# Attention and a two-layer product on one core: second exp sums moved ahead of the first-product tiles, and three smaller moves

## The chip, the cores and the metric

One core of a Trainium2 chip. The metric is device time in microseconds of one execution; before, three runs took 422.45, 422.8 and 423.35 us, a median of 422.8. The core's engines are TensorE (PE in the profile; its weight loads are PEld), VectorE (DVE), ScalarE (ACT), GpSimd (POOL) and SyncE (SP), which here only issues transfers. Each runs its own instructions in order, and they wait for each other by semaphores.

## What is computed

```python
# q, k, v: (8 batches, 12 heads, 448 tokens, 64)
scores = (1 / sqrt(64)) * q @ k.T
m = max(scores); e = exp(scores - m)
attn = e / (sum(e) + exp(-m) + 1e-9)
x = (attn @ v) laid out as (8 * 448 tokens, 768)
h = x @ w_in            # (3584, 2048), the "first product"
g = max(h, 0) ** 2
out = g @ w_out         # (3584, 768), the "second product"
```

The kernel leaves the maximum out of both halves of the fraction, so that it is exp(scores) / (1 + sum(exp(scores))); the 1e-9 is left out too. The sums over the keys are matmuls with a column of ones ("row sums"), after VectorE has added the four chunks of keys together.

## The kernel before

Heads go in pairs, six to a batch. Batches 0 and 1 are worked pair by pair; from batch 2 on two pairs make a cycle, three cycles a batch. In a cycle TensorE does the scores of two pairs (`ua`, `ub`), between them pieces of the second product of an earlier batch (`rows`), then the values of the cycle before, then tiles of the first product of the batch before (`run(ins, ...)`), and among them the row sums of its own two pairs. ScalarE takes the exps and the reciprocals (as exp(-ln)). VectorE adds the exp chunks, normalises the values into `xt`, and takes each first-product tile out of PSUM (maximum with 0 into `rt`, L296; square into `gs`, L298).

```python
def cast(b, pr):
    for name in "qk":
        f = flat.tile([P, 2, RUN, D], FP16, name=f"flat{name}")
        nc.vector.tensor_copy(f, naturals[name, b, pr])                     # L145
        naturals[name, b, pr] = f

def transposes(b, pr):
    tp = mp_tile(FP16)
    for i, name in enumerate("qk"):
        ...  # eight TensorE transposes each                                # L153
    nc.vector.tensor_copy(qks[b][:, 0:2, pr * S:(pr + 1) * S], tp[:, :, 0:S])   # L157

def add_chunks(u, et, es, half, step):       # for n == S
    e = et.rearrange("p (k x) -> p k x", k=RUN)
    if step < 2:
        nc.vector.tensor_add((es, half[:, 0:2 * S])[step], e[:, 2 * step], e[:, 2 * step + 1])  # L207
    else:
        nc.vector.tensor_add(es, es, half[:, 0:2 * S])                      # L209

def mp_tile(dtype=FP32):     # three buffers of m_psum and one of x_psum, in turn
    if joined[0] >= 0:
        joined[0] += 1
    pool, name = (x_psum, "xp") if joined[0] > 0 and joined[0] % 4 == 0 else (m_psum, "mp")
    return pool.tile([128, 512] if dtype == FP32 else [128, 2, 512], dtype, name=name)
```

`row_sums` takes such a tile, does two matmuls per unit into it (L243), and ScalarE's Ln (L246) and Exp (L247) make the reciprocals. `values` (L229) and `tile_in` (L279, 12 half-array matmuls per 128 columns of `w_in`) take such tiles too. `tile_out` does 384 output columns of 128 tokens in 16 matmuls (L326 split by rows, L281 on the whole array); ScalarE or VectorE takes them out, and SyncE stores them.

The start, where three and four warming matmuls (`keep_warm`, L420) stand around the first scores:

```python
keep_warm(9)
cast(0, 0)
transposes(0, 0)
keep_warm(3)
cast(0, 1)
for i in range(2 * NPAIR):
    ...
    scores(u, et, 0)
    if i == 0:
        keep_warm(4)
```

Batch 1's last part sets how much first product each of its pairs drains; `left()` is what is still queued:

```python
        if first:
            queue(FIRST, S - FIRST)
            share[0] = left() / (NPAIR + 0.9)
```

A cycle from batch 2 on:

```python
        scores(ua, ea, 0); rows(11)
        scores(ua, ea, 1)
        add_chunks(ua, ea, sa, ha, 0)
        rows(11)
        scores(ub, eb, 0)
        add_chunks(ua, ea, sa, ha, 1); add_chunks(ua, ea, sa, ha, 2)
        rows(10)
        scores(ub, eb, 1)
        add_chunks(ub, eb, sb, hb, 0)
        for at in pending:                 # the two pairs of the cycle before
            ...
            xp = mp_tile()
            values(units[at], ets.pop(at), xp)
            normalise([units[at]], xp, rcps.pop(at))
        if b in ON_PE and pr + 2 < NPAIR:  # batch 2 alone, here
            transposes(b, pr + 2)
            transposes(b, pr + 3)
        if pr == 0:
            run(ins, len(ins))
            queue((b - 1) * S, S)
            if b > 2:
                run(outs)
            ...  # transfers for the next batches
        n = (3, 7, 6)[pr // 2]
        early = (0 if b > 2 else 2) if pr == 0 else 3
        if pr:
            run(ins)                       # one tile
        add_chunks(ub, eb, sb, hb, 1)
        add_chunks(ub, eb, sb, hb, 2)
        run(ins, early - (pr > 0))
        for at in (i, i + 1):
            rcps[at] = row_sums([units[at]], (ess.pop(at)[0:1],))
        run(ins, n - early)
```

Of the kernel before, what the change touches and what calls it, by code (L numbers as in the profile page):

```python
# [10 lines left out]
AF = mybir.ActivationFunctionType  # L11
# [4 lines left out]
def kernel(  # L16
# [9 lines left out]
    nc = tc.nc  # L26

    B, H, S, D = q.shape
    NT, DM = out.shape
    DF = moe_w_in.shape[1]  # L30
    NPAIR = H // 2
    DCH = DM // 128
    NFFB = DF // 128
# [4 lines left out]
    HALF = DM // 2  # L38
# [36 lines left out]
    whole, vns, qks, xts, naturals, stages = {}, {}, {}, {}, {}, {}  # L75
# [66 lines left out]
    def cast(b, pr):  # L142
        for name in "qk":
            f = flat.tile([P, 2, RUN, D], FP16, name=f"flat{name}")
            nc.vector.tensor_copy(f, naturals[name, b, pr])  # L145
            naturals[name, b, pr] = f

    def transposes(b, pr):
        tp = mp_tile(FP16)
        for i, name in enumerate("qk"):  # L150
            for s in range(RUN):
                for h in range(2):
                    nc.tensor.transpose(tp[64 * h:64 * h + 64, i, P * s:P * s + P],  # L153
                                        naturals[name, b, pr][:, h, s, :], ident[0:P, 0:P])
        if b not in qks:
            qks[b] = qk_pool.tile([128, 3, COLS], FP16, name="qk")
        nc.vector.tensor_copy(qks[b][:, 0:2, pr * S:(pr + 1) * S], tp[:, :, 0:S])  # L157

# [41 lines left out]
    def add_chunks(u, et, es, half, step):  # L202
        n = u[3]
        if n == S:
# [5 lines that stand above are left out]
        elif step == 1:  # L210
            nc.vector.tensor_add(half[:, 0:4 * n], et[:, 0:4 * n], et[:, 4 * n:8 * n])
        elif step == 2:
            f = half[:, 0:4 * n].rearrange("p (h j n) -> p h j n", h=2, j=2)
            nc.vector.tensor_add(es[:, 0:2 * n].rearrange("p (h n) -> p h n", h=2), f[:, :, 0, :], f[:, :, 1, :])
# [35 lines left out]
    def normalise(us, xp, rcp):  # L250
        b, pr, q0, n = us[0]
        if b not in xts:
            xts[b] = xt_pool.tile([128, DCH, S], FP16, name="xt")
        if len(us) == 1:
            nc.vector.tensor_mul(xts[b][:, pr, q0:q0 + n], xp[:, 0:n], rcp[:, 0:n])
        else:
            two = [t[:, 0:2 * n].rearrange("p (j n) -> p j n", j=2) for t in (xp, rcp)]
            nc.vector.tensor_mul(xts[b][:, pr:pr + 2, q0:q0 + n], *two)
# [51 lines left out]
            nc.sync.dma_start(out=rows[t, p:p + m, :], in_=ot[o:o + m, n0:n1])  # L310
            c += m

    def tile_out(tok, n0):

        w = HALF
        if n0 == 0:
            ots[tok] = osb_pool.tile([128, DM], FP32, name="ot")
        ot = ots[tok]
        rows = mode[0] == ROWS2
        op = mp_tile()  # L320
        lo = mp_tile() if rows else None
        for fb in range(NFFB):
            g = gs[:, fb, tok % RING:tok % RING + 128]
            if rows:
                for x, o in ((0, op), (64, lo)):
                    nc.tensor.matmul(o[:, 0:w], g[x:x + 64], wout[x:x + 64, fb, n0:n0 + w],  # L326
                                     start=(fb == 0), stop=(fb == NFFB - 1))
            else:
                product(op[:, 0:w], g, wout[:, fb, n0:n0 + w], start=(fb == 0), stop=(fb == NFFB - 1))
            if fb < NFFB - 1:  # L330
                yield w / 2.4
        if rows and n0 == 0:
            nc.vector.tensor_scalar(out=ot[:, n0:n0 + w], in0=op[:, 0:w], scalar1=OUT_SCALE, scalar2=None, op0=ALU.mult)
        else:
            nc.scalar.activation(out=ot[:, n0:n0 + w], in_=op[:, 0:w], func=AF.Copy, scale=OUT_SCALE)  # L335
        if rows:
            nc.vector.scalar_tensor_tensor(out=ot[:, n0:n0 + w], in0=lo[:, 0:w], scalar=OUT_SCALE,  # L337
                                           in1=ot[:, n0:n0 + w], op0=ALU.mult, op1=ALU.add)
        last = tok + 128 == NT
        if n0 or last:  # L340
            store(tok, ot, n0 if last else 0, n0 + w)
        yield w / 2.4

# [25 lines left out]
    ins, outs = [], []  # L369
    groups = [0]  # L370
# [8 lines left out]
    def complete(upto):  # L379

        while groups[0] + 128 <= upto:
            for n0 in (0, HALF):
                ns = NFFB * HALF / 2.4
                outs.append([ns, ns, tile_out(groups[0], n0)])
            groups[0] += 128

    def left():
        return sum(t[0] for t in ins)
# [9 lines left out]
    def drain(ns):  # L398
        while ins and ns > 0:
            ns -= one(ins)  # L400

    def run(tiles, n=1):
        for _ in range(min(n, len(tiles))):
            for _ in tiles.pop(0)[2]:
                pass
# [16 lines left out]
    share = [0.0]  # L422
# [67 lines left out]
    for i in range(2 * NPAIR, 3 * NPAIR):  # L490
        u, et, es, half = begin(i)
        prev = units[i - 1]
        first = i == 2 * NPAIR
        if not first:
            xp = x_psum.tile([128, 512], FP32, name="xp")
        mode[0] = COLS2
        scores(u, et, 0)
        if i in transpose_at:
            transposes(*transpose_at[i])
        if i == 2 * NPAIR + 2:  # L500
            load_natural(2, 3, 6)
            for j in range(2):
                load_wout(HALF, j, 2)
            load_v(2, 0, 6)
            stage(3)
        drain(left() * 0.5 if first else share[0] * 0.45)
        scores(u, et, 1)
        if first:
            done = units[i - 2:i]
            values(prev, ets.pop(i - 1), xp, prev[3])  # L510
            rcp = row_sums(done, (ess.pop(i - 2)[0:1], ess.pop(i - 1)[0:1]))
        else:
            done = [prev]
            rcp = row_sums(done, (ess.pop(i - 1)[0:1],))
            values(prev, ets.pop(i - 1), xp)
        drain(share[0] * 0.15)
        for step in range(3):
            add_chunks(u, et, es, half, step)
            drain(share[0] * (0.15, 0.1, 0.15)[step])
        if i == 3 * NPAIR - 1 and ins and ins[0][0] < ins[0][1]:  # L520
            run(ins)
        normalise(done, xp, rcp)
        if first:
            queue(FIRST, S - FIRST)
            share[0] = left() / (NPAIR + 0.9)

# [11 lines left out]
    for c in range((NU - 3 * NPAIR) // 2):  # L540
        i = 3 * NPAIR + 2 * c
        b, pr = units[i][0:2]
        new = []
        for j in range(2):
            new.append(begin(i + j))
        (ua, ea, sa, ha), (ub, eb, sb, hb) = new
        scores(ua, ea, 0)
# [5 lines that stand above are left out]
        add_chunks(ua, ea, sa, ha, 1)  # L553
        add_chunks(ua, ea, sa, ha, 2)
# [3 lines that stand above are left out]
        mode[0] = COLS2  # L558
        for at in pending:
            if at not in rcps:  # L560
                rcps[at] = row_sums([units[at]], (ess.pop(at)[0:1],))
            xp = mp_tile()
            values(units[at], ets.pop(at), xp)
            normalise([units[at]], xp, rcps.pop(at))
        if b in ON_PE and pr + 2 < NPAIR:
            transposes(b, pr + 2)
            transposes(b, pr + 3)
# [5 lines that stand above are left out]
            if b + 1 < B:  # L573
                transposed_loads(b + 1)
                hold(b + 1)
                load_v(b + 1, 0, NPAIR)
                if b + 2 < B:
                    stage(b + 2)
        n = (3, 7, 6)[pr // 2]
        early = (0 if b > 2 else 2) if pr == 0 else 3  # L580
        if pr:
            run(ins)
        add_chunks(ub, eb, sb, hb, 1)
        add_chunks(ub, eb, sb, hb, 2)
        run(ins, early - (pr > 0))
        for at in (i, i + 1):
            rcps[at] = row_sums([units[at]], (ess.pop(at)[0:1],))
        run(ins, n - early)
        if pr == NPAIR - 2:
            complete(b * S)  # L590
        pending = [i, i + 1]
# [38 lines left out]
```

The softmax here doesn't subtract the row's maximum and nothing guards it: scores larger than these inputs give would overflow.

## Time and profile before

| what | value |
|---|---|
| time, median of three | 422.8 us |
| span of the profiled execution | 420.5 us |
| attention cycles (batch 2 to 7) | about 68 to 358 us |
| last batch's products alone | about 358 to 417 us |
| TensorE's granted clock | 1.00 in every stretch |
| last store, issued and landed | 417.5, about 419 us |

The page gives busy time by engine, the chain of work that ended last, and groups of instructions by source line. The trace behind it gives single instructions with start and duration, and for each idle stretch of an engine the instruction that ended it. An arrow `<-` in a tile's name separates what is written from what is read. `64*112` ahead of a shape is the part of the 128 x 128 array that a matmul uses; two such matmuls on different halves run side by side. A matmul's drawn end lies past the next one's start, since matmuls are pipelined.

### The profile page before, as it was taken

The numbers are of one execution on the slowest core, as the hardware profiler recorded it, in microseconds if no ns is written. First come the engines' busy times: TensorE is split into PE (matmuls) and PEld (weight loads), VectorE is DVE, ScalarE is ACT, GpSimd is POOL, SyncE is SP. The second block draws the span as 40 slices with busy tenths as digits, with TensorE's granted clock in tenths as the row PEclk, the third lists the DMA queues.
The fourth block names the chain that finished last, engine by engine and source line by source line (L and its number), as shares of the span: only waits on it lengthen the run. The fifth ranks groups of instructions, "written<-read, shape, count | busy, mean of one in ns | idle before, by whom it ended". The sixth has DMA issues, their size and how long they took to land.

```text
span 420.5 us, 10659 instructions
## 1 busy us (share of the span) xinstructions
PE 408.4 (97%) x4705; PEld 259.9 (62%) x4705; DVE 280.2 (67%) x535; ACT 237.8 (57%) x327; POOL 36.2 (9%) x58
## 2 busy tenths in 40 slices
PE   8889999899999999999999999999999999999996
PEld 3567666566666666666666666666666666655663
DVE  4769888677864967668766768568676669287000
ACT  3998997755566464764675664673666665100111
POOL 7523310020000200002000300001000000000000
PEclk9999999999999999999999999999999999999999
DMA  9999999889109940299409960198101101010222
GB/s 205 197 197 198 200 202 199 156 142 175 38 19 207 179 107 2 75 204 169 104 2 181 175 136 19 39 203 138 40 2 39 39 2 39 38 39 0 76 75 76
DMA packets 75679, 45.58 MB, mean 108 GB/s; under 512 B 42544, under 2 KB 71856, under 8 KB 75312
## 3 DMA queue, kind: packets, MB, share of 16 engines
q0 software_dynamic: 28848, 22.16, 34.6%
q1 hardware_dynamic: 46064, 22.05, 23.1%
q10 hardware_dynamic: 720, 0.69, 0.6%
q8 instruction: 37, 0.61, 0.6%
q14 instruction: 10, 0.08, 0.1%
HBM read 45.69 MB, written 17.93 MB: 151 GB/s over the span
## 4 chain that ended last, share of the span: by engine, by line
PE 82%; DVE 11%; ACT 5%; issue 1%; ACTq 0%
PE mp L279 20%; PE mp L326 17%; PE mp L281 10%; PE sp L194 6%; PE mp L229 5%; PE xp L279 5%; PE xp L326 5%; DVE rt L296 4%; PE xp L281 4%; ACT et L162 3%; PE xp L229 3%; PE sp L182 3%; DVE es L209 2%; DVE half L207 2%; PE mp L420 1%; DVE gs L298 1%
## 5 line engine op out<-in xcount | busy, mean ns | idle before, releaser
L162 ACT ACTIVATE et<-sp 112x896 f16<-112x896 f32 (+2 forms) x192 | 166.0, 914 | 61.5 <-PE sp L194 44.2
L279 PEld LDWEIGHTS <-win 128*64 128x64 f16 x1536 | 90.6, 110 | 43.3 <-issue 7.4
L279 PE MATMUL mp<-xt,win 128*64 128x448 f16 (+2 forms) x1248 | 111.8, 324 | 2.8 <-DVE rt L296 1.2
L326 PE MATMUL mp<-wout,gs 64*128 64x384 f16 x864 | 102.3, 323 | 0.0
L296 DVE TENSOR_SCALAR rt<-mp 128x448 f16<-128x448 f32 (+2 forms) x100 | 62.2, 622 | 28.1 <-PE mp L279 16.0
L326 PEld LDWEIGHTS <-gs 64*128 64x128 f16 x1152 | 56.0, 94 | 31.9
L298 DVE TENSOR_TENSOR gs<-rt 128x448 f16<-128x448 f16 (+2 forms) x128 | 50.2, 392 | 4.4
L326 PE MATMUL xp<-wout,gs 64*128 64x384 f16 x288 | 52.6, 323 | 0.0
L246 ACT ACTIVATE rcp<-mp,one_b 128x448 f32<-128x448 f32 (+2 forms) x39 | 24.5, 629 | 36.1 <-PE mp L243 36.1
L335 ACT ACTIVATE ot<-mp 128x384 f32<-128x384 f32 x28 | 13.8, 492 | 52.5 <-PE mp L281 41.5
L207 DVE TENSOR_TENSOR es<-et 112x896 f16<-112x896 f16 x42 | 26.0, 620 | 17.7 <-ACT et L162 17.7
L194 PE MATMUL sp<-qk 64*112 64x224 f16 x480 | 33.8, 260 | 0.0
L281 PEld LDWEIGHTS <-gs 128*128 128x128 f16 x240 | 23.4, 98 | 15.8 <-issue 0.4
L194 PEld LDWEIGHTS <-qk 64*112 64x112 f16 x480 | 26.3, 128 | 9.7 <-issue 5.4
L279 PE MATMUL xp<-xt,win 128*64 128x448 f16 x288 | 31.5, 353 | 0.5 <-DVE rt L296 0.5
L229 PEld LDWEIGHTS <-vn 112*64 112x64 f16 x432 | 22.3, 109 | 15.0 <-issue 5.1
L281 PE MATMUL mp<-wout,gs 128*128 128x384 f16 x176 | 29.4, 326 | 0.0
L337 DVE SCALAR_TENSOR_TENSOR ot<-mp,ot 128x384 f32<-128x384 f32 x26 | 14.5, 558 | 21.8 <-PE sp L194 13.5
L247 ACT ACTIVATE rcp<-rcp 128x448 f32<-128x448 f32 (+2 forms) x48 | 27.7, 577 | 1.5
L209 DVE TENSOR_TENSOR es<-es,half 112x896 f16<-112x896 f16 x42 | 26.3, 625 | 1.4
L207 DVE TENSOR_TENSOR half<-et 112x896 f16<-112x896 f16 x42 | 25.9, 617 | 0.3 <-ACT et L162 0.3
L182 PE MATMUL sp<-qk 64*112 64x448 f16 (+2 forms) x192 | 24.0, 321 | 1.9 <-ACT et L162 1.4
(60 smaller groups left out, 310.9 us busy)
## 6 DMA issues: line engine op xcount, KB each, us to landing
vn<-in_v_dram POOLq DMA_DIRECT2D x7, 672.0 KB, 8.0
out_dram<-ot SPq DMA_DIRECT2D x9, 384.0 KB, 2.9
win<-in_moe_w_in_dram POOLq DMA_DIRECT2D x8, 384.0 KB, 13.8
wout<-in_moe_w_out_dram POOLq DMA_DIRECT2D x4, 768.0 KB, 12.9
stage_q<-in_q_dram POOLq DMA_DIRECT2D x4, 676.0 KB, 10.6
stage_k<-in_k_dram POOLq DMA_DIRECT2D x4, 676.0 KB, 13.6
out_dram<-ot SPq DMA_DIRECT2D x8, 288.0 KB, 2.6
out_dram<-ot SPq DMA_DIRECT2D x10, 192.0 KB, 2.7
```

What stands on the lines that cost most here:

```text
L162: nc.scalar.activation(out=out_, in_=in_, func=AF.Exp, scale=scale)
L182: nc.tensor.matmul(sp[:, h, o:o + n], qk[r, 1, x + P * kk:x + P * kk + P], qk[r, 0, x + q0:x + q0 + n], start=True, stop=True)
L194: nc.tensor.matmul(sp[:, odd, h * (S // 2):(h + 1) * (S // 2)], qk[r, which, kx:kx + 2 * P - 1:2], qk[r, 0, x:x + S // 2], start=True, sto ...
L207: nc.vector.tensor_add((es, half[:, 0:2 * S])[step], e[:, 2 * step], e[:, 2 * step + 1])
L209: nc.vector.tensor_add(es, es, half[:, 0:2 * S])
L229: nc.tensor.matmul(xp[64 * h:64 * h + 64, o:o + n], vns[b][:, 2 * pr + h, kk, :], of_head(chunk(et, u, kk // 2, kk), u, h), start=(kk == 0 ...
L247: nc.scalar.activation(out=rcp[:, 0:m], in_=rcp[:, 0:m], func=AF.Exp, scale=-1.0)
L279: nc.tensor.matmul(out_[x:x + 64], lhsT[:, x:x + 64], rhs, start=start, stop=stop)
L281: nc.tensor.matmul(out_, lhsT, rhs, start=start, stop=stop)
L296: nc.vector.tensor_scalar(out=rt[:, 0:m], in0=hp[:, 0:m], scalar1=0.0, scalar2=None, op0=ALU.max)
L298: nc.vector.tensor_mul(gs[:, f0:f0 + per, t0 % RING:t0 % RING + n], r, r)
L326: nc.tensor.matmul(o[:, 0:w], g[x:x + 64], wout[x:x + 64, fb, n0:n0 + w], start=(fb == 0), stop=(fb == NFFB - 1))
```

## The change

Four edits. In a cycle, the second pair's last two adds (`add_chunks(ub, ..., 1)` and `2`) move to right behind the normalises, ahead of the qk copies and of every product tile; where a tile stood ahead of them, it now goes with the others, so that three tiles come before the row sums as before. At the seam from batch 1 to batch 2, batch 1's pairs drain a smaller share of the first product, so that a tile is left for the first cycle of batch 2, and that cycle does one new tile instead of two ahead of its row sums. At the start, ScalarE casts the first k while VectorE casts the first q, and the first copy of transposed q and k is made in two halves. At the end, the last 384 output columns are made as 256 and 128, each with its own copy and store.

```diff
@@ cast
-            nc.vector.tensor_copy(f, naturals[name, b, pr])
+            if b == 0 and pr == 0 and name == "k":
+                nc.scalar.activation(out=f, in_=naturals[name, b, pr], func=AF.Copy)
+            else:
+                nc.vector.tensor_copy(f, naturals[name, b, pr])
@@ transposes
-        nc.vector.tensor_copy(qks[b][:, 0:2, pr * S:(pr + 1) * S], tp[:, :, 0:S])
+        parts = (0, S // 2, S) if b == 0 and pr == 0 else (0, S)
+        for x, y in zip(parts, parts[1:]):
+            nc.vector.tensor_copy(qks[b][:, 0:2, pr * S + x:pr * S + y], tp[:, :, x:y])
@@ complete (tile_out takes its width w; cut)
-            for n0 in (0, HALF):
+            last = groups[0] + 128 == NT
+            for n0, w in ((0, HALF), (HALF, 256), (HALF + 256, 128)) if last else ((0, HALF), (HALF, HALF)):
@@ batch 1
-            share[0] = left() / (NPAIR + 0.9)
+            share[0] = left() / (NPAIR + 1.5)
@@ cycles
             normalise([units[at]], xp, rcps.pop(at))
+        add_chunks(ub, eb, sb, hb, 1)
+        add_chunks(ub, eb, sb, hb, 2)
         if b in ON_PE and pr + 2 < NPAIR:
 ... (cut)
-        n = (3, 7, 6)[pr // 2]
-        early = (0 if b > 2 else 2) if pr == 0 else 3
-        if pr:
-            run(ins)
-        add_chunks(ub, eb, sb, hb, 1)
-        add_chunks(ub, eb, sb, hb, 2)
-        run(ins, early - (pr > 0))
+        n, early = ((3, 0 if b > 2 else 1), (7, 3), (6, 3))[pr // 2]
+        run(ins, early)
         for at in (i, i + 1):
             rcps[at] = row_sums([units[at]], (ess.pop(at)[0:1],))
         run(ins, n - early)
```

More of the change, by code (lines that the diff above doesn't have):

```diff
@@ L311, in store, with tile_out @@
             c += m
-    def tile_out(tok, n0):
-        w = HALF
+    def tile_out(tok, n0, w):
         if n0 == 0:
@@ L339, in tile_out @@
         last = tok + 128 == NT
-        if n0 or last:
+        if n0 + w == DM or last:
             store(tok, ot, n0 if last else 0, n0 + w)
@@ L381, in complete @@
         while groups[0] + 128 <= upto:
-            for n0 in (0, HALF):
-                ns = NFFB * HALF / 2.4
-                outs.append([ns, ns, tile_out(groups[0], n0)])
+            last = groups[0] + 128 == NT
+            for n0, w in ((0, HALF), (HALF, 256), (HALF + 256, 128)) if last else ((0, HALF), (HALF, HALF)):
+                ns = NFFB * w / 2.4
+                outs.append([ns, ns, tile_out(groups[0], n0, w)])
             groups[0] += 128
```

## Prediction

> **What bounds the kernel now.** I read the engine shares first, then the chain that ended last, then TensorE's waits, then the timeline around one of them.
>
> ```profile
> span 420.5 us, 10659 instructions
> ...
> PE 408.4 (97%) x4705; PEld 259.9 (62%) x4705; DVE 280.2 (67%) x535; ACT 237.8 (57%) x327; POOL 36.2 (9%) x58
> ...
> PE 82%; DVE 11%; ACT 5%; issue 1%; ACTq 0%
> ```
>
> TensorE is the bound, and the chain is 82% TensorE. But 97% is an upper bound on how full it is: matmul records overlap, so a late matmul hides behind the drawn length of the one before. So I compared start to start: a block's time until the next block starts, against its columns at 2.4 per ns (warming matmuls of 512 columns start 216 ns apart), halved where two half-array matmuls run side by side. From 83 to 358 us (attention cycles) this gives dense blocks: 36 first-product matmuls of 448 columns should take 36 x 448 / 2.4 / 2 = 3,360 ns and take 3,408. What stands out are the row sums (L243). Their view of waits:
>
> ```profile
> its engine sat idle before it (us, times) until:
>   DVE es L209: 5.3, 14
> ```
>
> A stalled cycle, and one that isn't (columns: start, duration, engine, line, operation, tiles, count, idle before and who ended it):
>
> ```profile
> 160.02 0.63 DVE L209 TENSOR_TENSOR es<-es,half 112x896 f16<-112x896 f16 x1
> 160.27 0.11 PEld L243 LDWEIGHTS <-ones 112*64 112x64 f16 x2
> 160.46 0.62 PE L243 MATMUL mp<-es,ones 112*64 112x448 f16 x4
> ...
> 160.70 0.11 PEld L243 LDWEIGHTS <-ones 112*64 112x64 f16 x2 [0.31 <-DVE es L209]
> ...
> 161.23 1.11 PE L279 MATMUL mp<-xt,win 128*64 128x448 f16 x9 [0.15 <-DVE rt L296]
> ```
>
> ```profile
> 174.74 0.62 DVE L209 TENSOR_TENSOR es<-es,half 112x896 f16<-112x896 f16 x1
> ...
> 175.79 0.55 PE L243 MATMUL mp<-es,ones 112*64 112x448 f16 x4
> ...
> 176.17 0.74 PE L279 MATMUL mp<-xt,win 128*64 128x448 f16 x6
> ```
>
> Start of the sums to the next block: 161.23 - 160.46 = 0.77 us against 176.17 - 175.79 = 0.38 us. The first waits until the second unit's `es` ends at 160.65; in the second cycle it ended at 175.36, before the sums were reached. So the stall is 0.39 us. The same figure returns in 12 cycles: pairs 2 and 4 of batches 2 to 7. The cycles of pair 0 of batches 3 to 7 don't have it.
>
> **What the Trainium skill says.** "PSUM — Partial Sum Buffer", section "Engine vs sequencer instructions": VectorE's queue is strictly first in, first out, and matmuls start in program order. The trace agrees: `es` at 160.02 stands behind the eviction of a product tile that could not start before 158.40, and the sums behind the third tile. So where an add stands in VectorE's order is what matters. "TensorE: Matmul & The Clock Gate", section "Back-to-back issue gap": in a stream of weight load and matmul pairs the spacing is about 81 ns at 128 columns, not the 53 that the columns alone take. No block of before has 128-column matmuls on full weights, so no run shows it yet. "Perfetto Trace Analysis", section "Identifying the Most-Contended Engine": matmul busy share says little of how full TensorE is; the 97% beside about 37 us of start-to-start excess agrees.
>
> **Part 1, the second adds behind the normalises.** No instruction is added or removed. In pairs 2 and 4 VectorE ran: two normalises, eviction and square of product tile 1, the two adds, evictions of tiles 2 and 3. Now: normalises, adds, evictions. TensorE's order is the same: values, 3 tiles (one plus two before), sums, rest. In the cycle above the normalises end at 158.04, with a next start possible at about 157.95. The adds take 0.65 to their dependent start and 0.63, so `es` is ready at about 159.2, while tile 3 ends at 160.46: 1.2 us to spare. Does the delayed eviction bite? Tiles use four PSUM buffers in turn. Tile 1's eviction moves from 158.40 to about 159.13, tile 2's from 160.56 to 160.1, tile 3's from 161.53 to 161.0. Sum 2 takes tile 1's buffer (free at 159.8, wanted at 160.65), tile 4 takes tile 2's (free at 160.7, wanted at 160.85). No new wait. In pair 2 of batch 2 two qk copies (0.53 apart) also stand between, and tile 4 waits perhaps 0.05. Sum: 12 x 0.39 = **4.7 us off**, all on the path, because TensorE has only dense work around it. For pair 0 of batches 3 to 7 no tile stood ahead of the adds before either, so nothing changes.
>
> **Part 2, the seam.** A batch-1 share is now left / 7.5 instead of left / 6.9. In TensorE's order, 22 of the 44 matmuls (256 columns) at 65.52 move, with two more from an earlier unit, into one tile after the first transposes of batch 2. 22 x 256 / 2.4 / 2 = 1.17 us goes from a place where ScalarE had just run out of work to the seam:
>
> ```profile
> 77.31 2.79 PE L279 MATMUL mp<-xt,win 128*64 128x448 f16 x24 [0.46 <-ACT rcp L246]
> 79.90 0.38 PE L243 MATMUL mp<-es,ones 112*64 112x448 f16 x2
> 80.83 0.38 PE L243 MATMUL xp<-es,ones 112*64 112x448 f16 x2 [0.55 <-DVE es L209]
> 81.05 1.30 PE L279 MATMUL mp<-xt,win 128*64 128x448 f16 x12
> 82.28 0.58 PE L182 MATMUL sp<-qk 64*112 64x448 f16 x4
> ```
>
> There TensorE waits for a Ln to free a buffer, then for the last normalise, then for `es`. I replayed it with the durations of before. Everything from 65.5 on starts 1.17 us earlier, so the kept tile starts at 76.14 (the buffer still waits for the Ln) and ends at 77.42, where the normalise is done. The first 448 tile ends at 78.55. `es` is now ready at about 78.54. But VectorE does the adds before the two qk copies, so these end at 79.06 and 79.59, and the sums need exactly their buffers: 79.1 and 79.65. The next tile needs the kept tile's eviction, behind the copies, at 80.2. It starts at 80.25, and two tiles (2.28) end at 82.5, against 82.28 before. So the wait changes its name from `es` to buffers, and the seam is worth **+0.2 us**, with a replay error of about 0.5 either way.
>
> **Part 3, the start.** The k cast leaves VectorE (0.41 us there) and becomes a ScalarE copy of 512 columns. From the exps, (1019 - 807) / 256 = 0.83 ns a column, it should take 807 - 256 x 0.83 = 0.6 us. k lands at about 4.6, so it ends near 5.2.
>
> ```profile
> 4.94 0.41 DVE L145 CAST flatk<-et 112x512 f16<-112x512 f32 x1
> ...
> 5.40 0.39 PE L153 MATMUL mp<-ident,flatk 112*64 112x112 f16 x8
> ...
> 5.72 0.82 PE L420 MATMUL mp<-warm 128*128 128x512 f16 x3
> 5.83 0.63 DVE L157 COPY qk<-mp 128x896 f16<-128x896 f16 x1 [0.48 <-PE mp L153]
> ...
> 6.51 0.18 PEld L182 LDWEIGHTS <-qk 64*112 64x112 f16 x4 [0.46 <-DVE qk L157]
> ```
>
> The k transposes start behind the q ones at 5.40 either way. The copy in two halves lets the first scores start once the first half is there, about 6.05, but three warming matmuls hold TensorE until about 6.36. So 0.15 at most, and about **-0.1 us** on the path.
>
> **Part 4, the last tile.** Its second half becomes 256 and 128 columns. At the end stand one ScalarE copy of 0.49 us and a store:
>
> ```profile
> 416.96 0.49 ACT L335 ACTIVATE ot<-mp 128x384 f32<-128x384 f32 x1 [2.06 <-PE mp L281]
> ```
>
> The last copy shrinks by 256 x 0.83 ns = 0.21 us, and the last store from 192 to 64 KB. By size the median to landing runs from 2.3 (96 KB) to 2.7 (192 KB) but 3.0 at 48 KB, so I estimate 0.2 us. Against this, 16 more weight loads: at the skill's 81 ns, 16 x (81 - 53) = 0.45 us more. Sum **0.0**.
>
> Total: -4.7 + 0.2 - 0.1 + 0.0 = -4.6; 422.8 - 4.6 = **418.2 us**, 1.1% faster.
>
> **Rivals.** (a) A buffer wait takes the place of the `es` wait: delayed evictions make sum 2 or tile 4 wait in every cycle. The seam shows that the buffers bind when two copies stand ahead; in the 11 cycles without a copy the margins are 0.15 to 0.9 us. If it happened in all, 0.15 of each 0.39 would be lost, about 420.0. (b) ScalarE or VectorE becomes the bound once TensorE stops waiting: busy 57 and 67% of the span, and 60 and 72% from 83 to 358 us, with idle at each cycle's end, so unlikely; it would leave 420 or more. (c) The seam is better than replayed, because the tile fills the Ln wait: up to 1 us less, 417.2. (d) Narrow matmuls are slower than estimated at the end: at 98 ns (a weight load's duration in the trace) 0.7 instead of 0.45, so 418.5. DMA is no rival: the second half of w_out has landed at 64.5, before the seam, and later DMA is light.
>
> **Range and chances.** Part 1 carries all. Its spread is about 0.6, the seam's 0.5, start and tail's 0.4 each, runs of before differ by 0.9. So 417.0 to 419.8. A 2% gain needs 414.3, which not even all stalls together with the best seam give; 2% slower needs a wait of 0.5 us in every cycle.
>
> **What would show it.** Right: the wait of L243 on `es` falls from 5.3 us to under 1; sums to next block 0.38 us in all cycles after the seam; cycles of pair 2 and 4 0.39 shorter and those of pair 0 unchanged. Seam: sums that wait for the qk copy, scores of the next cycle near 82.4. Start: first exp at 6.8 instead of 6.93. Tail: 16 matmuls of 128 columns in about 1.3 us. Wrong would be: new waits on L296 or L157 in the cycles, or a first exp that comes later because ScalarE's cast does.

## The result, and the profile after

| | median, us | runs |
|---|---|---|
| before | 422.62 | 422.34 to 423.35 |
| changed | 417.74 | 417.68 to 417.88 |

The ratio is 0.988, 95% interval 0.9865 to 0.9899: 4.9 us off, inside the range and 0.5 us under the point. But of the four parts only the first two came out close, and that the errors of all four cancelled is luck. The page of the changed kernel, the lines that answer to those of before (line numbers are up to five higher):

```profile
span 415.9 us, 10695 instructions
...
PE 405.5 (98%) x4721; PEld 256.7 (62%) x4721; DVE 278.8 (67%) x535; ACT 238.4 (57%) x329; POOL 36.4 (9%) x58
...
PE 86%; DMA 9%; ACT 2%; DVE 2%; issue 1%; POOL 0%; POOLq 0%
```

VectorE has gone from 11% of the chain to 2%: the waits on `es` are out of it. DMA has come in with 9%, which was not expected; it is the subject of the third part below. The view of the row sums (L248 now), and a cycle that stalled before:

```profile
its engine sat idle before it (us, times) until:
  issue: 3.5, 12
  DVE qk L162: 0.7, 2
```

```profile
156.57 1.15 DVE L260 TENSOR_TENSOR xt<-mp,rcp 128x448 f16<-128x448 f32 x2
...
158.28 0.63 DVE L214 TENSOR_TENSOR es<-es,half 112x896 f16<-112x896 f16 x1
158.83 0.62 DVE L301 TENSOR_SCALAR rt<-mp 128x448 f16<-128x448 f32 x1
...
160.15 0.55 PE L248 MATMUL mp<-es,ones 112*64 112x448 f16 x4
...
160.53 0.73 PE L284 MATMUL xp<-xt,win 128*64 128x448 f16 x6
```

`es` ends at 158.91, 1.2 us before the sums, and from the sums to the next block is 160.53 - 160.15 = 0.38 us, the figure of an undisturbed cycle.

To see where the rest went I set the two traces side by side, block by block on TensorE, and noted by how much each block comes later or earlier than the same block before ("drift").

| stretch | drift at its end | change in it |
|---|---|---|
| to the transposes at 38 us | +0.39 | +0.39 |
| to 65 us | +0.50 | +0.11 |
| seam, to the scores at 83.1 | +0.83 | +0.33 |
| cycles, to the last batch's products at 355.5 | -4.07 | -4.90 |
| end of the span | -4.66 | -0.59 |

### The profile page after: what moved, and what is told of

Read it like the earlier page. It is cut to its first block, busy times and chain, and to the rows that moved or that the text cites. A ratio compares the mean times of both kernels' runs of the same rounds, so it can differ in the third digit from the quotient of the medians.

```text
span 415.9 us, 10695 instructions
## 1 busy us (share of the span) xinstructions
PE 405.5 (98%) x4721; PEld 256.7 (62%) x4721; DVE 278.8 (67%) x535; ACT 238.4 (57%) x329; POOL 36.4 (9%) x58
## 4 chain that ended last, share of the span: by engine, by line
PE 86%; DMA 9%; ACT 2%; DVE 2%; issue 1%; POOL 0%; POOLq 0%
PE mp L284 23%; PE mp L330 17%; PE mp L286 11%; PE xp L284 8%; PE sp L199 6%; PE xp L330 6%; PE mp L234 5%; DMA kn<-in_k_dram 4%; PE xp L286 3%; DMA win<-in_moe_w_in_dram 3%; PE xp L234 3%; PE sp L187 2%; DMA vn<-in_v_dram 2%; PE mp L248 2%; ACT et L167 1%
## 5 line engine op out<-in xcount | busy, mean ns | idle before, releaser
L284 PEld LDWEIGHTS <-win 128*64 128x64 f16 x1536 | 85.3, 110 | 45.7 <-issue 2.8
L284 PE MATMUL mp<-xt,win 128*64 128x448 f16 (+2 forms) x1236 | 110.2, 324 | 1.5 <-DVE xt L263 0.8
L339 ACT ACTIVATE ot<-mp 128x384 f32<-128x384 f32 (+1 forms) x29 | 14.1, 487 | 36.2 <-PE mp L286 27.6
L286 PEld LDWEIGHTS <-gs 128*128 128x128 f16 x256 | 24.4, 98 | 15.1 <-issue 0.4
L284 PE MATMUL xp<-xt,win 128*64 128x448 f16 x300 | 32.6, 352 | 0.0
L286 PE MATMUL mp<-wout,gs 128*128 128x384 f16 (+1 forms) x192 | 31.0, 322 | 0.0
L301 DVE TENSOR_SCALAR rt<-xp 128x448 f16<-128x448 f32 x29 | 18.0, 622 | 12.0 <-PE xp L286 8.3
```

Of the source, the lines that this page charges most:

```text
L284: nc.tensor.matmul(out_[x:x + 64], lhsT[:, x:x + 64], rhs, start=start, stop=stop)
L286: nc.tensor.matmul(out_, lhsT, rhs, start=start, stop=stop)
L301: nc.vector.tensor_scalar(out=rt[:, 0:m], in0=hp[:, 0:m], scalar1=0.0, scalar2=None, op0=ALU.max)
```

## The experiments

Each kernel was timed beside the kernel before on the same chip; the ratio is to that kernel, with its 95% interval. Single runs of one kernel differ by up to 5 us (422.24 to 427.39 for the kernel before), so below half a microsecond the drift in the profiles says more than the medians. A drift is that of one execution.

### One part at a time

**e1**: only the moved adds, without the first cycle of batch 2 (`c` is the cycle's number).

```diff
+        ahead = c > 0
+        if ahead:
+            add_chunks(ub, eb, sb, hb, 1); add_chunks(ub, eb, sb, hb, 2)
         ...
-        add_chunks(ub, eb, sb, hb, 1)
-        add_chunks(ub, eb, sb, hb, 2)
+        if not ahead:
+            add_chunks(ub, eb, sb, hb, 1); add_chunks(ub, eb, sb, hb, 2)
```

> Only the moved adds, in every cycle but the first of batch 2. Theory: the row sums lose their wait on es, 0.39 us in each of 12 cycles, so the time falls by 4.7 us (to about 417.9) and the wait of the sums on es nearly goes from the profile. Rival, a buffer wait takes over part of it: 2 to 3 us off and new waits on the product tile's eviction.

417.94 us, ratio 0.988 (0.9868 to 0.9893). In its profile the drift falls from +0.68 to -4.23 over the cycles, 4.91 us: eleven steps of about 0.42, and 0.32 in the first. This part alone makes the change. The wait on `es` that is left is the one of the first cycle, at 81 us, where the adds still stand behind the copies (0.98 us of it lie before the weight load and 0.55 before the matmul, counted as two):

```profile
its engine sat idle before it (us, times) until:
  issue: 2.3, 10
  DVE es L209: 1.5, 2
  DVE es L214: 0.4, 1
```

**e2**: only the smaller share and the first cycle's new order.

```diff
-            share[0] = left() / (NPAIR + 0.9)
+            share[0] = left() / (NPAIR + 1.5)
```

with `ahead = c == 0` in the form of e1, and `early` 1 instead of 2 there.

> Only the smaller share in batch 1 and the first cycle of batch 2 in its new order. My replay said +0.2 us; the two traces, taken apart, say +0.4 (the scores of the next cycle come 0.83 later, of which 0.39 was there before the seam). Rival, the kept tile fills the wait on the Ln: up to 1 us faster.

423.48 us, ratio 1.0008 (0.9996 to 1.002): not told from nothing by the time. The profile puts it at +0.45 us (0.11 near 65 us, 0.34 at the seam), as in the changed kernel. It isn't faster, so the rival falls.

**e3**: only the start, as in the diff of the change.

> Only the k cast on ScalarE and the copy in halves. Prediction: 0.1 us faster. Theory now: the k of batch 1's second half lands at about 38 us and the transposes wait for it in both kernels, so nothing earlier counts and the time is the same within 0.1 us; the first exp comes 0.1 us later than before, not earlier. Rival: the start itself delays everything, 0.1 to 0.4 us slower, also after 38 us.

422.63 us, ratio 0.9992 (0.9982 to 1.0001), which tells nothing this small. The first exp starts at 7.12 us, not earlier than the 6.93 of before. The start also differs between executions for another reason (the last section), so only like ones can be compared: the drift at 12 us is 0.00 and 0.01 in e4 and e8, which have the old start, and 0.10 and 0.20 in the changed kernel and its repetition e11, all four with the full clock on record before 5.0 us. So the start edits cost 0.1 to 0.2 us in those two executions. The three lines below are from the timeline of the changed kernel:

```profile
4.86 0.63 ACT L146 ACTIVATE flatk<-et 112x512 f16<-112x512 f32 x1 [1.34 <-DMA et<-in_k_dram]
...
5.54 0.24 PEld L156 LDWEIGHTS <-flatk 112*64 112x64 f16 x8 [0.23 <-ACT flatk L146]
...
7.03 0.81 ACT L167 ACTIVATE et<-sp 112x768 f16<-112x768 f32 x1 [1.54 <-PE sp L187]
```

The first k landed at 4.84, TensorE waits for ScalarE's cast, and the k transposes start at 5.54 instead of 5.40. In e11 it landed at 4.93, and they start at 5.64. But in e3 itself it landed at 4.66, the cast ran from 4.68 to 5.31, and nothing waited for it: its drift at 12 us, 0.19, lies between the 0.14 and 0.24 of e2 and e1, which have the old start and the full clock about as late. So this cost depends on the landing, which came between 4.55 and 4.97 us in the fourteen profiles. The copy in two halves gave little: the first scores start 0.09 us after the columns of the last warming matmul (216 ns from its start) in the changed kernel, e3, e6 and e11, and 0.13 after them before and in e4 and e8. No run separates the two start edits.

**e4**: only the small last tile, as in the diff of the change.

> Only the small last tile. Prediction: no change, since 128-column matmuls at 81 ns would give back 0.45 us. By the trace of the changed kernel: 16 narrow matmuls take hardly more than their columns, the last copy is 0.21 shorter and the last store about 0.3 shorter, so 0.5 us faster.

422.11 us, ratio 0.998 (0.9973 to 0.9987): 0.8 us off, by the profile 0.6. The end of the changed kernel:

```profile
411.84 1.06 PE L286 MATMUL xp<-wout,gs 128*128 128x128 f16 x16
...
412.93 0.28 ACT L339 ACTIVATE ot<-xp 128x128 f32<-128x128 f32 x1 [0.51 <-PE xp L286]
```

From the last copy's start to the end of the span it is 415.87 - 412.93 = 2.94 us, against 420.53 - 416.96 = 3.57 before.

### What holds the kernel at 38 us

In the first six profiles (before, changed, e1 to e4) one transfer, the k of the second half of batch 1, landed between 37.90 and 38.67 us, in kernels that differ before that point by the start edits at most. In five of them TensorE's transposes of it began 0.04 to 0.05 us later: they waited for it. In e2, where it landed first, they began 0.11 later and right behind those of q (0.22 us from start to start), without a wait. In the changed kernel the chain of waits shows it (start, duration, what):

```profile
10.31 12.93 DMA win<-in_moe_w_in_dram
...
23.82 14.56 DMA kn<-in_k_dram
38.38 0.04 issue
38.42 0.39 PE mp L156 x8
```

Before, it landed at 37.99 and its transposes began at 38.03: the wait was there as well (0.38 us from the start of the q transposes to that of the k ones), but so short that the chain went another way. **e5** takes it away by order alone:

```diff
-    for i in range(4, 8):
+    for i in range(4, 6):
         load_win(i, 8)
     load_natural(1, 3, 6)
+    for i in range(6, 8):
+        load_win(i, 8)
```

> The kernel before with one move in GpSimd's order of transfers: batch 1's second half of q and k ahead of the last two pieces of w_in instead of behind them. Theory: in all six profiles so far the transposes near 38 us start 0.04 to 0.05 us after that k has landed (37.9 to 38.7 us from run to run), so the transfer bounds what comes before. Landing about 4 us earlier, the transposes start as soon as TensorE gets there (about 37.85) and the time falls by 0.2 to 0.8 us. Rival: the last two pieces of w_in, now 3 to 4 us later, make the first product wait instead; no change or slower.

422.67 us, ratio 0.9992 (0.9981 to 1.0002): no gain that the time can tell. The k now lands at 34.95, long before its transposes. But in this execution the matmuls between 6 and 10 us came 1.07 us later (last section), late enough that the old order wouldn't have waited either, so its profile doesn't show the gain. It does show that the later pieces of w_in make nothing wait: past 38 us the drift stays at +0.88 to +0.85 to the last batch. e8, below, shows the gain.

**e6**: the start edits on top.

> The start edits on top of the moved transfers. If the transfer was what hid the start, this shows its own worth against the moved transfers alone: by its profile the first exp isn't earlier, so 0 to 0.1 us slower than those. The prediction's step would want 0.1 us faster.

422.40 us, ratio 0.9988 (0.9972 to 1.0003), against 0.9992 for e5. The times don't settle what the start edits are worth once the transfer is out of the way, and the two profiles began differently, so this stays open. In e6's profile k landed at 4.55 and its cast ended at 5.20, as the prediction had it; the first exp starts at 6.93, as before, though the full clock is on record 0.45 us later (5.39 against 4.94). Against the edits stand the 0.1 to 0.2 us above, where k landed later.

### What the kept tile costs at the seam

**e7**: the smaller share alone; the first cycle keeps its old order and its two tiles ahead of the sums.

> Half of the seam edit: batch 1 keeps a tile, but the first cycle of batch 2 leaves its adds behind the qk copies and does two new tiles ahead of the sums, as before. Theory of the replay (buffers bind at the seam): the copies end 1.3 us earlier than in the full seam edit, so the second new tile gets its buffer at once; sums then wait for es and the kept tile's eviction at about 80.2. The scores of the next cycle come 0.9 us earlier than in the full seam edit and 0.5 us earlier than before: 422.4, against 423.5 for the full edit. Rival, the kept tile itself costs what was measured: no better than the full edit.

423.14 us, ratio 1.0 (0.9988 to 1.0013). The expectation failed: by the drift this costs 0.30 us (+0.87 to +1.17), only 0.15 less than e2. The timeline shows why:

```profile
78.75 0.61 DVE L157 COPY qk<-xp 128x896 f16<-128x896 f16 x1
79.28 0.68 DVE L296 TENSOR_SCALAR rt<-mp 128x512 f16<-128x512 f32 x1
79.99 0.43 DVE L298 TENSOR_TENSOR gs<-rt 128x512 f16<-128x512 f16 x1
80.33 0.62 DVE L207 TENSOR_TENSOR half<-et 112x896 f16<-112x896 f16 x1
80.99 0.63 DVE L209 TENSOR_TENSOR es<-es,half 112x896 f16<-112x896 f16 x1
...
81.67 0.38 PE L243 MATMUL mp<-es,ones 112*64 112x448 f16 x2 [0.62 <-DVE es L209]
```

I had put the adds ahead of the kept tile's eviction and square; in the program they stand behind them. VectorE works here without a break, and the order only chooses who waits: `es` here, the buffers in e2. That made a new theory: the kept tile moves 1.17 us of TensorE's work to the seam, but also 1.05 us of VectorE's, to the one place where VectorE is what TensorE waits for. **e9** and **e10** take load from VectorE there:

```diff
-        nc.vector.tensor_copy(qks[b][:, 0:2, pr * S:(pr + 1) * S], tp[:, :, 0:S])
+        dst = qks[b][:, 0:2, pr * S:(pr + 1) * S]
+        if b == 2 and pr in (2, 3):
+            nc.scalar.activation(out=dst, in_=tp[:, :, 0:S], func=AF.Copy)
+        else:
+            nc.vector.tensor_copy(dst, tp[:, :, 0:S])
```

> The seam edit of e2 with the two copies on ScalarE. If VectorE's load, with one more product tile to take out, was what the kept tile cost, the scores of the next cycle come 1.0 to 1.2 us earlier than in e2, and the time is about 422.3 against e2's 423.5. If the kept tile is bad for another reason (TensorE's waits on the Ln and on buffers), about 423.2.

422.24 us, ratio 0.9982 (0.9967 to 0.9998), against 423.48 for e2. Compare the seam of the changed kernel, first, with that of e10:

```profile
76.60 2.64 PE L284 MATMUL mp<-xt,win 128*64 128x256 f16 x36 [0.46 <-ACT rcp L251]
79.59 0.38 PE L248 MATMUL mp<-es,ones 112*64 112x448 f16 x2 [0.36 <-DVE qk L162]
80.12 0.38 PE L248 MATMUL xp<-es,ones 112*64 112x448 f16 x2
80.72 2.46 PE L284 MATMUL mp<-xt,win 128*64 128x448 f16 x24 [0.22 <-DVE rt L301]
```

```profile
77.14 2.63 PE L283 MATMUL mp<-xt,win 128*64 128x256 f16 x36 [0.46 <-ACT rcp L250]
77.61 0.90 ACT L159 ACTIVATE qk<-mp 128x896 f16<-128x896 f16 x1
...
78.41 0.91 ACT L159 ACTIVATE qk<-xp 128x896 f16<-128x896 f16 x1
...
79.59 0.38 PE L247 MATMUL mp<-es,ones 112*64 112x448 f16 x2
79.78 0.38 PE L247 MATMUL xp<-es,ones 112*64 112x448 f16 x2
...
80.21 2.46 PE L283 MATMUL mp<-xt,win 128*64 128x448 f16 x24
```

From the kept tile's start to the last two tiles it is 80.21 - 77.14 = 3.07 us, against 80.72 - 76.60 = 4.12: 1.05 us. Of this 0.54 lies ahead of the first sums, where the wait for the qk copy is gone, 0.34 between the two sums, and 0.17 behind them, where the next tile still waits for an eviction, but less long. By the drift the seam edit, which cost 0.45 us, is now 0.61 to the good. Of this the copies alone, without the kept tile, bring 0.33 (e9, below); the other 0.28 is the kept tile's. So VectorE's load at the seam was what made the tile a cost. The rival was no part of it: the wait on the Ln is 0.46 us in both.

### Put together

**e8**: the adds as in e1, the last tile, the transfers of e5.

> What helped, together: the adds in every cycle but batch 2's first, the small last tile, the moved transfers; neither the start edits nor the kept tile. If the parts add up, 422.8 - 4.8 - 0.6 - 0.4 = 417.0, below the full change's 417.7; if they don't, 417.5 or more.

416.87 us, ratio 0.9867 (0.9828 to 0.9905): by the median the parts add up. Here the start was that of before (drift 0.01 at 12 us), the k landed at 34.47, and its transposes follow those of q at once:

```profile
37.66 0.39 PE L153 MATMUL mp<-ident,qn 112*64 112x112 f16 x8
...
37.88 0.36 PE L153 MATMUL mp<-ident,kn 112*64 112x112 f16 x8
```

From the q transposes to the k ones it is 0.22 us, without a wait, against 0.38 before, and over this stretch the drift falls by 0.19 us. The changed kernel, where k landed at 38.38, is then 0.57 us behind e8, 0.09 of it from before this stretch. DMA's share of the chain is 1%, against 9% there.

**e9**: e8 with ScalarE's two copies.

> The three helpful parts of e8 and, new, the two qk copies of batch 2's first cycle made by ScalarE instead of VectorE. Theory: from the last normalise of batch 1 on VectorE works without a break, and that is what TensorE waits for at the seam; ScalarE waits there for 2.4 us and does the two copies (about 0.9 us each) in that time. The replay puts the scores of the next cycle 0.8 us earlier: 416.1 against e8's 416.9. Rival, ScalarE's Ln of the row sums falls behind the copies and gives it back: the same as e8.

416.89 us, ratio 0.986 (0.9847 to 0.9873), no faster than e8 by the medians, on another chip. The second sums come 0.74 us earlier by the drift, but 0.41 goes back in the next cycle, whose exps start behind a later Ln and Exp:

```profile
82.24 0.62 ACT L250 ACTIVATE rcp<-xp,one_b 128x448 f32<-128x448 f32 x1
82.89 0.58 ACT L251 ACTIVATE rcp<-rcp 128x448 f32<-128x448 f32 x1
83.37 3.32 ACT L166 ACTIVATE et<-sp 112x896 f16<-112x896 f32 x4
```

The scores of these exps start at 82.33, so the exps come 1.04 us behind them, against 0.44 before (82.28 and 82.72). The rival had its part; 0.33 us is left.

**e11**: the change as it is, beside e9 and e10.

> The whole change on the chip of e9 and e10, so that they can be compared on one chip: 417.7 as at first, 0.8 above e8's time and 1.6 above what e9 should take. If e9 is no faster than this, the parts left out of it cost nothing.

417.64 us, ratio 0.9878 (0.9866 to 0.9891). e9, on the same chip, is 0.75 lower by the medians, but that doesn't tell what the parts left out cost from what the moved transfers and the copies bring.

**e12**: the adds in every cycle, the smaller share, ScalarE's copies, the last tile and the moved transfers; the start as before the change.

> The change without its start edits, with the moved transfers and with the two copies on ScalarE. By the profiles of e9 and e10 the kept tile with ScalarE's copies is worth 0.6 us at the seam and e9's form 0.3 net, so 416.6 here against 416.9 for e8 and e9. Rival: the late Ln of e9 shows here as well, and it stays at 416.9.

416.55 us, ratio 0.9853 (0.984 to 0.9867), as expected. The late Ln of e9 doesn't show: the first exps of the next cycle start 0.44 us behind their scores again (82.46 and 82.02). It is the lowest of all: 6.4 us under the kernel before. Against the change, 417.7, it is 1.1 to 1.2 lower by the medians, on different chips, and the two intervals just touch.

## Why the prediction was right, and where not

**Part 1, right.** 12 stalls, 4.7 us; measured 4.90 in the change and 4.91 in e1. Eleven of the stalls gave 0.42 instead of 0.39: behind the stalled sums, up to the next scores, the matmuls on one half of the array also started 0.03 us after those on the other, and now they start together. The first, in pair 2 of batch 2, gave 0.32: behind the two qk copies there, 0.07 us passes after its sums that passes in no other cycle, where the prediction had 0.05. No other wait took the place of the old ones, so rival (a) falls in the cycles; nor did VectorE or ScalarE become the bound there (b).

**Part 2, the sign right, the size too small.** Of 0.44 us, 0.33 is the seam, within the error of 0.5 that the replay gave itself. Corrected for the drift of 0.50 that was there before it, the replay's points hold to a tenth: sums at 79.09 (79.1), the next tile at 80.22 (80.25), the scores at 82.61 (82.5). It missed 0.11 us near 65 us, where the sums of batch 1's last pair wait a little longer for a qk copy. The cause given, buffers behind the copies, was the surface; e7 and e10 showed VectorE's load below it. Rival (c) falls as the edit was made.

**Part 3, wrong three times.** The step "k lands at about 4.6, so it ends near 5.2", with the k transposes at 5.40 "either way", took one landing for fixed: k landed at 4.84 and the cast ran from 4.86 to 5.49, past the end of the q transposes, so TensorE waits for it. The sign of being wrong that the prediction named came true: the first exp starts at 7.03 us, later than the 6.93 of before, because the cast ends later. The step "0.15 at most" took TensorE for free as soon as the warming matmuls are through; the first scores come 0.09 us after that, against 0.13 with the whole copy, so that the halved copy is worth about 0.04. (e3 and e6, where k landed early enough, had the full clock later than before; their first exps start at 7.12 and 6.93.) And the sentence "DMA is no rival" looked at w_out alone. In six of the nine profiles with the old order of transfers one of them holds TensorE at 38 us, so that a tenth at the start, won or lost, doesn't reach the end; the +0.39 at 38 us in the changed kernel is this landing (38.38 against 37.99), which varied by more (37.90 to 38.67) between executions of kernels with the old start.

**Part 4, a mis-sized term.** I took 16 x (81 - 53) = 0.45 us from the Trainium skill, "TensorE: Matmul & The Clock Gate", section "Back-to-back issue gap". In the trace the 128-column matmuls start 55.8 ns apart with a weight load for each, and those of 256 columns 109.1: all 32 cost 0.04 us more than before. The measurement decides here; the same section's formula for single matmuls, 128 / 2.4 + 2.5, fits it. The last copy gave 0.21 us as computed (0.49 to 0.28), and the last store 0.35 instead of 0.2 (issue to landing 1.88 to 1.53). Another 0.06 lies between that landing and the end of the span (1.18 to 1.12). Sum -0.59 instead of 0.0. The rival (d), slower narrow matmuls, falls.

So the sum was -4.6 and the span changed by -4.66, but the terms were -4.90, +0.44, +0.39 (not the change's doing) and -0.59.

## What to carry to other kernels

When an operation feeds a wait of the busiest engine, and its own inputs are there, put it in its engine's queue ahead of work whose input comes later: here the adds stood behind an eviction whose tile wasn't finished, nothing was added or removed, and 1.2% came off. Before work is moved into a gap of the busiest engine, count what it drags along on the others: the gap at the seam was VectorE's making, and a tile that filled it brought VectorE more to do. A gain before the point where a transfer lands is only worth something once that transfer lands earlier, and the wait can be missed where it is short in the one execution that was profiled.

## What the runs showed of the hardware

The first microseconds differ between executions of the same instructions. Three warming matmuls and their wait at the start took 0.79 us from start to the next block before, but 1.21 in e5, and by 10 us the drift was 1.07:

```profile
6.04 1.28 PE L422 MATMUL mp<-warm 128*128 128x512 f16 x3
7.25 0.37 PE L182 MATMUL sp<-qk 64*112 64x192 f16 x4
```

In e5's trace the record of the full TensorE clock starts at 7.0 us, in that of the kernel before at 4.9, and the rate of the warming matmuls changes there: those three start 0.40 and 0.43 us apart in e5, and the four at 7.55 then 0.22 to 0.23; before, the nine from 1.20 on start 0.40 to 0.43 apart, and the three at 5.72 already 0.22 to 0.23. (So the clock of 1.00 "in every stretch", given for the kernel before, doesn't hold for its first 4.9 us.) This slower rate accounts for the 0.42 us between 0.79 and 1.21. Over the fourteen profiles the record starts between 4.2 and 7.2 us, and the four with the largest drift at 12 us, 0.95 to 1.12, are the four where it starts last, at 6.85 or later. That it makes the rest of that drift is likely but not shown, and what sets its moment no run here shows.

The last store varies too: with the same instructions it took 1.88 to 1.89 us from issue to landing before and in e1, e2, e3, e6 and e7, but 2.96 in e5 and 2.73 in e10.
